# Two blocks of q and k in one load each, turned by head: one pair of a 24-block attention and FFN kernel

## The chip, the cores and the metric

The kernel runs on one core of a Trainium2 chip. The metric is the device time in microseconds (us), the median of several executions; beside it stands one execution that the hardware profiler recorded, on which the trace and the page are based.

## The reference

Two stages. The first is attention over 4 batches of 768 tokens with 8 heads of 64, where a query sees the last 96 keys and the first 8 of its batch, with a bias that falls with the distance at a slope of its own for each head. The second is a two-layer FFN with softplus over the 3072 rows of 512 that the attention gives.

```python
scores = scale * np.matmul(q, k.transpose(0, 1, 3, 2))
keep = is_global | is_local              # k < 8, or 0 <= q - k < 96
scores = np.where(keep, scores - slopes * dist, -1e9)
a = np.exp(scores - max);  a = a / (sum(a) + 1e-09)
attn = np.matmul(a, v)                   # 4 x 8 x 768 x 64
x = attn.transpose(0, 2, 1, 3).reshape(3072, 512)
h = x @ w_in                             # 512 -> 2048
g = np.maximum(h, 0.0) + np.log1p(np.exp(-np.abs(h)))
out = g @ w_out                          # 2048 -> 512
```

q, k, v and the weights come as float32; the matrices are multiplied in bf16 (attention) and fp16 (FFN).

## The kernel before, in words

**Attention** goes by blocks of 128 tokens, 24 of them, six to a batch. A block's q, k and v are loaded by `load` (L100): 128 tokens on the partitions, 8 heads of 64 beside each other, cast to bf16 on the way, in DMAs that POOL issues. `tr_qk` (L254, step `t`) turns q and k on PE, a pair of heads at a time as a 128x128 product with the identity, into one PSUM bank `tr`; `qt_copy` and `kt_copy` (steps `qc`, `kc`) bring it to SBUF as `QT` and `KT`. From block 8 on `dma_qk` (step `d`) has SP's queue do this by a DMA transpose instead. Only block 0 is loaded on the SP and ACT queues and cast on the chip (`cq`, `ck`, `tq`, `tk`).

A block is worked in two halves of four heads. For blocks 0 to 3 the bias is laid into PSUM by a product with the identity (`z`, L299), into the bank pair `s_ps` for heads 0 to 3 and `oo` for heads 4 to 7, and the scores (`s`, L321, made by `qk`, L277) are added on top of it; ACT takes the Exp straight from there (`e`). Each key block serves two query blocks, its own and the next. P.V is `p` (L367), the division by the sums `norm` (`nm`, two DVE instructions that write `xsf`), and the turned result goes to `XT`, for blocks 0 to 7 through PE (`x` and the copy `xc`), from block 8 on through a DMA transpose on SP's queue (`y`). The first 8 tokens of a batch are copied over rows of later key blocks by `gk` and `gv`. The number behind the dot in these steps is the half, and for the copies the engine: 0 DVE, 1 ACT, 2 POOL.

**The FFN** goes by chunks of 256 tokens, two blocks each, 12 of them. Chunks 0 and 1 are done directly: `f` (L428) is one group of 256 hidden columns, `fe` and `lp` its softplus on ACT, `o` the second layer. The other chunks use a seven-product scheme on half-size blocks: `ht` (`x_dif`, L503) makes differences of `XT` on DVE, `h` (L528) the products of the first layer, `hc`, `hv`, `he`, `hl` what follows them, `gs` sums of G on DVE, `m` (L645) the products of the second layer, `ec`, `ev` the evictions and `st` the stores on SP's queue.

**The order of the work** is written out by hand: the string `ORDER` (L707) names one step after another, and each step issues its instructions at once on its engines, in that order; `BANKS` (L187) says which of three PSUM banks each short-lived tile takes. An engine works its instructions strictly in the order given. POOL's DMAs go over eight semaphores in turn, so a load also waits until the eighth before it has landed. A load step `lq6` is q of block 6; `g` steps are tiny POOL copies that hold the loads behind them back until ACT has come to a certain place.

Of the kernel before, what the change touches and what calls it, by code (L numbers as in the profile page):

```python
# [10 lines left out]
ALU = mybir.AluOpType  # L11
# [9 lines left out]
def kernel(  # L21
# [51 lines left out]
    q_r = [const.tile([P, H, D], BF16, name=f"q_t{n}") for n in range(RQK)]  # L73
    k_r = [const.tile([P, H, D], BF16, name=f"k_t{n}") for n in range(RQK)]
# [42 lines left out]

    def load_q(n):
        load(n, q, q_t)

    def load_k(n):
        load(n, k, k_t)
# [56 lines left out]
    def bias_part(half, part):  # L179
# [8 lines left out]
        "01201201210212012012012012102101200220201011021010112121010212210101211202210221"  # L188
        "011020201002110121120202112001221002"
# [37 lines left out]
    def copy_by(act):  # L227
        return nc.scalar.copy if act else nc.vector.tensor_copy

    def to_QT(n, tr, copy):  # L230
        QT[n] = work4.tile([P, NPAIR, P], BF16, tag="QT", name="QT", bufs=6)
        copy(QT[n][:], tr[:, 0, :, :])
# [9 lines left out]
    def dma_qk(n):  # L242

        QT[n] = work4.tile([P, NPAIR, P], BF16, tag="QT", name="QT", bufs=6)
        KT[n] = work4.tile(
            [P, NPAIR, P], BF16, tag="KT0" if n == first_of(n) else "KT", name="KT",
            bufs=2 if n == first_of(n) else 6,
        )
        nc.sync.dma_start_transpose(QT[n][:], q_t[n][:].rearrange("p h d -> p (h d)"))
        nc.sync.dma_start_transpose(KT[n][:], k_t[n][:].rearrange("p h d -> p (h d)"))  # L250
# [7 lines left out]

    def qt_copy(n, by_act=0):
        to_QT(n, TR[n], copy_by(by_act))  # L260

    def kt_copy(n, by_act=0):
        to_KT(n, TR[n], copy_by(by_act))
# [239 lines left out]
    def x_dif(c, i):  # L503
# [8 lines left out]
        nc.vector.tensor_tensor(HD[c, i][:], a, b, ALU.subtract)  # L512
# [89 lines left out]
    def w_dif_part(i, part):  # L602
# [9 lines left out]
        nc.vector.tensor_tensor(t[i], a, b, ALU.subtract)  # L612
# [5 lines left out]
    def g_sum(c, i):  # L618
# [8 lines left out]
        nc.vector.tensor_tensor(SM[c, i][:], a(), b(), op)  # L627
# [74 lines left out]
    def gate(s):  # L702
# [5 lines left out]
        cq0 lk1 w18 bb1.1 ck0 tq0 lq1 lv0 lk2 tk0 z0.0 lq2 z0.1 lv1 lq3 s0.0 s0.1 bb1.0 bb0.1  # L708
        e0.1 t1 qc1.0 kc1.0 lk3 bb0.0 lv2 z1.1 e0.0 p0.1 s1.1 z1.0 s1.0 e1.1 nm0.1 gk2.1 t2 e1.0
        lk4 p0.0 z2.0 nm0.0 lq4 lv3 qc2.0 p1.1 wi1 p1.0 wi3 kc2.0 nm1.0 wi0 nm1.1 gv2.2 x0 s2.0  # L710
        z2.1 s2.1 t3 e2.0 z3.0 e2.1 gk3.2 p2.0 qc3.0 kc3.0 nm2.0 s3.0 p2.1 lk5 xc0.0 gv3.2 z3.1
        e3.0 s3.1 gk4.2 e3.1 nm2.1 x1 x2 t4 lq5 wi2 p3.0 xc1.0 lv4 wi4 p3.1 qc4.0 kc4.1 f1 xc2.1
        fe1 nm3.0 wo0 nm3.1 s4.0 lv5 x3 wi6 f3 xc3.0 fe3 f9 ab4.0 s4.1 fe9 ab4.1 f0 wo1 t5 kc5.0
        e4.0 f8 qc5.0 gk5.1 s5.0 fe0 f2 ab5.0 f11 fe8 e4.1 gv4.0 wo2 fe2 e5.0 s5.1 fe11 f10 lp0
        p4.0 f13 hw1.0 fe10 hw2.0 f5 fe13 f4 lp1 nm4.0 p4.1 ab5.1 fe4 nm4.1 e5.1 fe5 hw3.0 f12
        gv5.2 x4 p5.0 lp4 nm5.0 o0 p5.1 lq6 nm5.1 xc4.0 lk6 hw1.1 wo3 fe12 o4 x5 f15 xc5.0 lp6
        wd1.0 f14 lp5 f7 ht2.1 fe14 fe15 lk7 h2.1.0 ht2.2 lq7 o1 hw4.0 wd1.1 fe7 hw3.1 hw2.1 lv6
        ht2.4 lq8 hc2.1.0.1 hw4.1 f6 h2.6.0 lp7 gs1.1 wd3.0 gs1.3 h2.2.0 fe6 lp2 o5 gs1.2 ht2.3
        h2.5.0 lp3 hc2.5.0.1 lk8 lk9 o2 o6 he2.11.0 hv2.6.0 t6 lv7 kc6.1 wd2.0 wd4.0 h2.7.0 o7
# [24 lines left out]
        h5.4.0 ec3.4.1 ac14.0 he5.12.0 h5.1.1 hl4.1.1 he5.21.0 g37 lq16 y12 m3.2.0 lv15 nm13.1
        hc5.1.1.1 e14.1 gs4.1 ev3.2 lq17 ab14.0 h5.5.1 h5.2.1 gv14.2 hc5.5.1.1 h5.6.1 hv5.6.1
        he5.11.1 y13 gk15.2 gs4.3 st2.0 m4.1.0 e14.0 ss15 hl5.0.0 h5.7.1 h5.3.1 gk16.2 ec4.1.1
        lq18 ac15.0 p14.0 d16 he5.12.1 gs4.2 hv5.7.1 ac15.1 h6.1.0 hl5.0.1 gv13 g43 nm14.0
        hc6.1.0.1 lk18 gs5.3 m4.6 ht6.1 ec4.6.1 ht6.3 h5.4.1 he5.21.1 he5.22.1 m4.2.1 g31 p14.1
        h6.2.0 he6.11.0 lv17 ht6.2 d17 ab15.0 m4.7 gs4.4 h6.5.0 nm14.1 g29 h6.6.0 ev4.2 he5.22.0
# [52 lines left out]
    def cast_q(n):  # L802
        nc.vector.tensor_copy(q_t[n][:], q_f)
# [68 lines left out]
```

## Time and profile before

| | |
|---|---|
| median of the runs | 202.66 us (202.66, 202.66 and 203.97) |
| the profiled execution | 203.91 us, its span 201.8 us |
| granted TensorE clock | 0.997 |
| PE busy | 194.4 us, 96% |
| DVE, ACT busy | 173.8 and 173.5 us, 86% each |
| POOL busy | 85.3 us, 42% |
| DMA packets | 110622, 101760 of them under 512 B |

The span runs from the first to the last instruction of the profiled execution, and 2.1 us of its time lie around it. In rows of the trace a line is that of the kernel file, `out<-in` names the tiles, and a time in brackets is how long the engine had stood before the first instruction of the row, with what it had waited for. The length of a PE row holds the way of the last product through the array, so rows overlap; what a product costs in a stream is read from the start of one row to the start of the next.

### The profile page before, as it was taken

What the parts mean: (1) busy time and instruction counts of PE and PEld (TensorE: products, weight loads), DVE (VectorE), ACT (ScalarE), POOL (GpSimd) and SP (SyncE); (2) the same over time, 40 slices, a digit from 0 to 9 for tenths busy, and PEclk for the clock granted to TensorE, in tenths of its full rate; (3) what the DMA queues carried; (4) which work ended last, traced back from release to release, by engine and by line L of the source; (5) the groups of instructions that cost most, each with busy time, mean ns of one, the idle gap of its engine ahead of it and who ended that gap; (6) DMA issues with size and microseconds to landing.
All of it is one profiled execution on the core that took longest, in us unless ns stands there. A gap on an engine that the chain in (4) does not pass through costs nothing.

```text
span 201.8 us, 6676 instructions
## 1 busy us (share of the span) xinstructions
PE 194.4 (96%) x2729; PEld 167.9 (83%) x2729; DVE 173.8 (86%) x403; ACT 173.5 (86%) x278; POOL 85.3 (42%) x142
## 2 busy tenths in 40 slices
PE   7989999999999999999999999989999999999993
PEld 2657887867989989989998998969999999999992
DVE  7557776999999999989999999979999998867571
ACT  2767699989999999999999999997999998898700
POOL 8997906860574648095264835451003110000000
PEclk9999999999999999999999999999999999999998
DMA  8999999999999999999999999999442512601123
GB/s 126 153 156 169 149 196 207 188 173 158 149 115 157 120 174 195 102 158 158 157 161 180 168 177 167 100 119 145 100 133 44 94 29 30 209 3 54 54 71 138
DMA packets 110622, 26.91 MB, mean 133 GB/s; under 512 B 101760, under 2 KB 108288, under 8 KB 110592
## 3 DMA queue, kind: packets, MB, share of 16 engines
q0 software_dynamic: 78080, 13.37, 98.3%
q1 hardware_dynamic: 31472, 12.85, 36.8%
q8 instruction: 21, 0.34, 0.7%
q10 hardware_dynamic: 1040, 0.26, 0.6%
q14 instruction: 9, 0.07, 0.2%
HBM read 27.26 MB, written 6.29 MB: 166 GB/s over the span
## 4 chain that ended last, share of the span: by engine, by line
PE 59%; DVE 20%; ACT 11%; DMA 5%; issue 3%; DVEq 0%; ACTq 0%
PE o L657 24%; PE hT L541 12%; PE p_ps L541 6%; PE hT L434 5%; PE x_ps L380 3%; DMA XT<-xsf 3%; ACT e_sb L571 3%; DVE sum L627 3%; ACT Pb L364 3%; PE s_ps L284 2%; DVE Z L353 2%; DMA k_f<-in_k_dram 2%; ACT G L575 2%; DVE w_dif L612 2%; DVE xsf L398 2%
## 5 line engine op out<-in xcount | busy, mean ns | idle before, releaser
L575 ACT ACTIVATE G<-e_sb 128x1024 f16<-128x1024 f32 x40 | 41.7, 1061 | 0.1
L541 PEld LDWEIGHTS <-w_sum 128*128 128x128 f16 x640 | 39.0, 98 | 3.2 <-issue 0.9
L364 ACT ACTIVATE Pb<-Z 128x1024 bf16<-128x1024 f32 (+1 forms) x40 | 39.9, 1002 | 0.0
L657 PEld LDWEIGHTS <-sum 128*128 128x128 f16 x352 | 32.7, 98 | 4.3 <-issue 0.6
L657 PE MATMUL o<-w_dif,sum 128*128 128x256 f16 x264 | 33.8, 273 | 0.6 <-DVE b L686 0.5
L541 PEld LDWEIGHTS <-w_in 128*128 128x128 f16 x480 | 29.4, 98 | 0.7 <-DMA XT<-xsf 0.2
L657 PEld LDWEIGHTS <-G 128*128 128x128 f16 x272 | 24.9, 98 | 3.1 <-issue 0.2
L571 ACT ACTIVATE e_sb<-hT 128x512 f32<-128x512 f32 x40 | 24.0, 602 | 2.9 <-PE hT L541 2.6
L541 PE MATMUL hT<-x_dif,w_sum 128*128 128x128 f16 x320 | 24.4, 219 | 0.3 <-DVE hT L551 0.3
L541 PE MATMUL hT<-XT,w_in 128*128 128x128 f16 x320 | 24.4, 219 | 0.0
L344 DVE TENSOR_TENSOR Z<-s_ps,biasA 128x1024 f32<-128x1024 f32 x19 | 23.1, 1216 | 1.1 <-PE s_ps L284 1.1
L275 POOL COPY v_t<-v_t 8x520 bf16<-8x520 bf16 x13 | 8.4, 645 | 33.7 <-PE x_ps L380 32.6
L657 PE MATMUL o<-w_out,G 128*128 128x256 f16 x168 | 21.8, 273 | 0.0
L102 POOL DMA_DIRECT2D v_t<-in_v_dram x24 | 21.5, 896 | 0.6 <-issue 0.5
L102 POOL DMA_DIRECT2D q_t<-in_q_dram x23 | 20.6, 895 | 2.2 <-DMA w_out<-in_moe_w_out_dram 1.4
L102 POOL DMA_DIRECT2D k_t<-in_k_dram x23 | 20.6, 900 | 1.6 <-issue 0.8
L398 DVE TENSOR_TENSOR xsf<-x_ps,rcp 128x256 f16<-128x256 f32 x44 | 18.7, 424 | 1.5
L380 PEld LDWEIGHTS <-Pb 128*128 128x128 bf16 x352 | 15.3, 98 | 2.5 <-issue 0.9
L380 PE MATMUL x_ps<-v_t,Pb 128*128 128x65 bf16 x324 | 17.1, 193 | 0.1
L434 PE MATMUL hT<-XT,w_in 128*128 128x256 f16 x128 | 15.6, 273 | 0.0
L566 DVE TENSOR_TENSOR e_sb<-hp,hT 128x512 f32<-128x512 f32 x20 | 13.6, 682 | 2.3 <-PE hT L541 2.3
L627 DVE TENSOR_TENSOR sum<-G 128x1024 f16<-128x1024 f16 x22 | 15.1, 687 | 0.0
(113 smaller groups left out, 381.4 us busy)
## 6 DMA issues: line engine op xcount, KB each, us to landing
out_dram<-osb SPq DMA_DIRECT2D x18, 256.0 KB, 4.1
v_t<-in_v_dram POOLq DMA_DIRECT2D x24, 128.0 KB, 5.9
k_t<-in_k_dram POOLq DMA_DIRECT2D x23, 128.0 KB, 5.9
q_t<-in_q_dram POOLq DMA_DIRECT2D x23, 128.0 KB, 5.8
w_out<-in_moe_w_out_dram POOLq DMA_DIRECT2D x4, 512.0 KB, 11.2
out_dram<-osb SPq DMA_DIRECT2D x10, 128.0 KB, 2.0
w_in<-in_moe_w_in_dram POOLq DMA_DIRECT2D x4, 256.0 KB, 7.1
w_in<-in_moe_w_in_dram POOLq DMA_DIRECT2D x2, 512.0 KB, 9.1
```

The lines of the kernel that those rows point to most:

```text
L102: nc.gpsimd.dma_start(dst[n][:, :, 0:D], src[b, :, i * P : (i + 1) * P, :].rearrange("h s d -> s h d"))
L344: nc.vector.tensor_tensor(Z[:], buf[:, 0:8, :], biasA[:, half, :, :], ALU.add)
L364: nc.scalar.activation(Pb[:, 0:nreg, :], src, AF.Exp, scale=inv_sqrt)
L380: nc.tensor.matmul(x_b[:, lh, :], Pb[:, r, :], v_t[n - t][:, h, :], start=(t == 0), stop=(t == 1 or first),)
L398: nc.vector.tensor_tensor(xsf[:, h0 : h0 + 4, :], x_b[:, :, 0:D], rcp[:, h0 : h0 + 4][:, :, None].to_broadcast([P, 4, D]), ALU.mult,)
L434: nc.tensor.matmul(hT[:, j, :], w[:, m, fo : fo + P], XT[c][:, m, :], start=(j == 0 and m == 0), stop=(m == KM - 1), skip_group_check=(j > 0),
L541: nc.tensor.matmul(o[:, b, :], lhs(k, b), rhs[:, k, :], start=(i in (1, 5) and b == 0 and k == 0), stop=(k == KH - 1), skip_group_check=True,)
L566: nc.vector.tensor_tensor(t, HS[c, "p", u][:], HT[c, "x", u][:], ALU.add)
L571: nc.scalar.activation(o, t, AF.Exp)
L575: nc.scalar.activation(g_tile(c)[:, b0 : b0 + HB, :], HS.pop((c, i, u))[:], AF.Ln, bias=1.0)
L627: nc.vector.tensor_tensor(SM[c, i][:], a(), b(), op)
L657: nc.tensor.matmul(o, lhs[:, k, :], rhs(k)[:, c0:c1], start=(i in (1, 2, 5) and k == 0), stop=(k == NU - 1), skip_group_check=(i not in (1 ...
```

## The change

q of blocks 2 and 3 (tokens 256 to 511 of the first batch) is loaded in one DMA, and so is k. Partition s of the tile holds the neighbouring tokens 2s and 2s + 1, so that for each head 128 numbers lie together in memory rather than 64. The tiles of q and k are made for two blocks each, and the tiles of the single blocks are halves of them. Such a pair can't be turned two heads at a time; `tr_pair` turns it by head and by token parity, 16 transposes of 128x64 for q and as many for k, where two blocks had 8 for q and 8 for k. The copy to `QT` and `KT` (`out_of`) puts the two parities back together: it reads the PSUM bank in steps, 64 tokens of one and 64 of the other parity in turn. The arithmetic is the same.

`ORDER` and `BANKS` are new as a whole. The steps are the same but for `lq3`, `lk3`, `t2` and `t3`, which are gone, and `tQ2` and `tK2`, which are new; some 30 small copies have moved between ACT, DVE and POOL. `sum_by` lets three kinds of sums run on POOL, but no step asks for it.

```diff
-    q_r = [const.tile([P, H, D], BF16, name=f"q_t{n}") for n in range(RQK)]
-    k_r = [const.tile([P, H, D], BF16, name=f"k_t{n}") for n in range(RQK)]
+    q_p = [const.tile([P, 2 * H, D], BF16, name=f"q_t{n}") for n in range(RQK // 2)]
+    k_p = [const.tile([P, 2 * H, D], BF16, name=f"k_t{n}") for n in range(RQK // 2)]
+    q_r, k_r = ([t[n // 2][:, H * (n % 2) : H * (n % 2) + H, :] for n in range(RQK)] for t in (q_p, k_p))
...
+    PAIRED = (2,)
+
+    def pair_of(t, n):
+        return t[n % RQK // 2][:].rearrange("p (h t) d -> p h t d", t=2)
+
+    def load_pair(n, src, t):
+        b, i = divmod(n, BPB)
+        nc.gpsimd.dma_start(
+            pair_of(t, n), src[b, :, i * P : (i + 2) * P, :].rearrange("h (s t) d -> s h t d", t=2)
+        )
+
     def load_q(n):
-        load(n, q, q_t)
+        if n in PAIRED:
+            load_pair(n, q, q_p)
+        else:
+            load(n, q, q_t)
...
+    def tr_pair(n, t, which):
+        tr = TR[which, n] = any_bank([P, 2, NPAIR, P], BF16, f"tr_{which}")
+        src = pair_of(t, n)
+        for j in range(2):
+            for h in range(H):
+                rows = slice(D * (h % 2), D * (h % 2) + D)
+                nc.tensor.transpose(tr[rows, j, h // 2, :], src[:, h, j, :], ident[:])
+
+    def out_of(which, n, copy):
+        half = P // 2 * (n % 2)
+        src = TR[which, n - n % 2][:, :, :, half : half + P // 2].rearrange("p t m s -> p m s t")
+
+        return lambda dst, _: copy(dst.rearrange("p m (s t) -> p m s t", t=2), src)
...
-        cq0 lk1 w18 bb1.1 ck0 tq0 lq1 lv0 lk2 tk0 z0.0 lq2 z0.1 lv1 lq3 s0.0 s0.1 bb1.0 bb0.1
-        e0.1 t1 qc1.0 kc1.0 lk3 bb0.0 lv2 z1.1 e0.0 p0.1 s1.1 z1.0 s1.0 e1.1 nm0.1 gk2.1 t2 e1.0
+        lk1 cq0 w18 bb1.0 lq1 z0.1 lq2 ck0 tq0 lv0 bb1.1 z0.0 tk0 s0.1 e0.1 lk2 s0.0 t1 kc1.0
+        lv1 qc1.0 lk4 z1.1 tQ2 s1.1 bb0.1 qc2.0 lq4 p0.1 e0.0 qc3.0 bb0.0 lv2 e1.1 p0.0 z1.0 wi1
...
```

209 lines of the change are left out of this document (110 added, 99 removed).

## The prediction

> **What bounds the kernel now.** I read the windows first, stage by stage. Columns: length, busy time (and count) of PE, of its weight loads, of DVE, of ACT and of POOL, then clock, mean DMA engines at work, GB/s.
>
> ```profile
> 0.00:10.00 10.00, 8.56 (x49) 4.15 (x51) 6.34 (x33) 5.22 (x12) 9.09 (x15) 1.00 1.60 139
> 10.00:20.00 10.00, 9.22 (x153) 6.40 (x150) 6.64 (x23) 6.73 (x9) 8.65 (x14) 1.00 1.91 163
> 20.00:50.00 30.00, 29.82 (x347) 23.00 (x345) 25.71 (x56) 26.76 (x43) 16.04 (x20) 1.00 1.70 179
> 50.00:130.00 80.00, 79.26 (x1253) 72.18 (x1248) 77.78 (x170) 78.24 (x127) 43.49 (x76) 1.00 1.89 154
> 130.00:140.00 10.00, 9.14 (x147) 8.14 (x145) 8.30 (x20) 8.65 (x13) 4.72 (x9) 1.00 2.09 137
> 140.00:190.00 50.00, 50.00 (x721) 46.65 (x719) 43.19 (x93) 46.70 (x76) 3.30 (x10) 1.00 0.29 70
> 190.00:201.80 11.80, 8.44 (x86) 7.40 (x83) 5.90 (x14) 1.21 (x3) 0.00 (x0) 0.96 0.32 113
> ```
>
> PE is the bound from 20 us to 190 us: it idles 0.18 + 0.74 + 0.86 + 0 = 1.8 us in 170. The last stretch ends with the same products, evictions and stores in both orders. So a new order can win at most those 1.8 us, and whatever the first 20 us hold; there POOL is the busiest engine (9.09 and 8.65 of 10), because it issues the loads one after another.
>
> Then PE, ACT and POOL in order of time through that head (start, length, instructions):
>
> ```profile
> 0.78 4.00 PE L800 MATMUL x_ps<-const-bfloat16-1.0 128*128 128x512 bf16 x9 [0.78 <-PEq L853]
> 5.35 0.61 PE L223 MATMUL tr<-ident,q_t 128*128 128x128 bf16 x4 [0.58 <-DVE q_t L803]
> ...
> 7.98 0.61 PE L223 MATMUL tr<-ident,q_t 128*128 128x128 bf16 x4
> 8.38 0.63 PE L223 MATMUL tr<-ident,k_t 128*128 128x128 bf16 x4
> 8.81 1.00 PE L310 MATMUL oo<-biasA,ident 128*128 128x512 bf16 x2
> 9.64 0.29 PE L380 MATMUL x_b<-v_t,Pb 128*128 128x65 bf16 x4
> 9.87 0.40 PE L284 MATMUL oo<-QT,KT 64*128 64x128 bf16 x8
> 10.20 0.60 PE L310 MATMUL s_ps<-biasA,ident 128*128 128x512 bf16 x2
> 10.74 0.40 PE L284 MATMUL s_ps<-QT,KT 64*128 64x128 bf16 x8
> 11.07 0.40 PE L223 MATMUL tr<-ident,q_t 128*128 128x128 bf16 x4
> 11.30 0.39 PE L223 MATMUL tr<-ident,k_t 128*128 128x128 bf16 x4
> 11.52 0.29 PE L380 MATMUL x_ps<-v_t,Pb 128*128 128x65 bf16 x4
> 12.41 0.59 PE L310 MATMUL s_ps<-biasA,ident 128*128 128x512 bf16 x2 [0.60 <-ACT Pb L364]
> 12.84 0.40 PE L380 MATMUL x_b<-v_t,Pb 128*128 128x65 bf16 x8
> 19.25 1.04 PE L434 MATMUL hT<-XT,w_in 128*128 128x256 f16 x8
> 20.23 0.40 PE L284 MATMUL s_ps<-QT,KT 64*128 64x128 bf16 x8
> ```
>
> Lengths hold the drain, so costs are read from start to start. Two bias products took 0.83 (8.81 to 9.64), later 0.54 (10.20 to 10.74) and 0.43 (12.41 to 12.84): PE runs at half rate until about 9.8, though the granted clock reads 1.00. Four transposes took 0.43 then (8.38 to 8.81), and 0.23 and 0.22 at full rate: 0.107 and 0.056 us each. The 0.11 between 0.54 and 0.43 is what changing between whole-array products and the 64-row ones of the scores costs.
>
> ```profile
> 10.31 1.03 ACT L364 ACTIVATE Pb<-oo 128x1024 bf16<-128x1024 f32 x1 [0.53 <-PE oo L284]
> ...
> 14.15 1.02 ACT L364 ACTIVATE Pb<-s_ps 128x1024 bf16<-128x1024 f32 x1 [1.78 <-PE s_ps L284]
> ...
> 17.92 1.02 ACT L364 ACTIVATE Pb<-oo 128x1024 bf16<-128x1024 f32 x1
> 2.37 0.88 POOL L102 DMA_DIRECT2D q_t<-in_q_dram  x1
> ...
> 11.90 2.33 POOL L108 DMA_DIRECT2D w_in<-in_moe_w_in_dram  x3
> ```
>
> The head is one chain: load, transposes, copy, bias and scores on PE, Exp on ACT (1.02 each), the bank free again for the next bias.
>
> **The change part by part: loads.** Four issues of 0.88 become two. A w_in issue steps 0.74 for 256 KB against 0.88 for 128 KB, so issue time goes by pieces, not bytes; a pair has as many pieces as one block had (128 by 8). I take 0.88 a pair: 1.75 us of POOL saved (none, if it went by bytes). Landing, from the tile views of q_t up to 12 us and of w_in up to 14 us:
>
> ```profile
> DMA to landing us min/median/max: 4.5/4.6/4.6
> DMA to landing us min/median/max: 6.8/7.3/7.9
> ```
>
> Counting on from 2.37, the q pair is issued at 3.24 and lands between 7.8 (as q_t) and 10.5 (as w_in); I take 8.3, nearer the rows with equally many small pieces. The first w_in, now tenth in the queue instead of thirteenth, goes out at 9.30 instead of 11.90 and lands 2.6 us sooner. But PE idles 0.18 us in 20 to 50, so earlier weights are worth 0.2 at most later on.
>
> **Transposes.** 16 of 128x128 become 32 by head, each half as wide in its weights and still 128 columns long: 32 x 0.056 − 16 x 0.056 = +0.9, and four changes of tile shape at 0.11, +0.4. The trace has no transpose of 64 columns; the ends are 0.041 (eight 64-row scores in 0.33, 9.87 to 10.20) and 0.107 each. I take 0.056, the same operation. What counts is where they stand. On PE, between the bias of block 1's second half (z1.1) and its scores (s1.1), before:
>
> ```order
> L310 LDWEIGHTS ident
> L310 MATMUL oo<-biasA,ident 128x512
> ...
> L380 LDWEIGHTS Pb
> L380 MATMUL x_b<-v_t_90,Pb 128x65
> ...
> L284 LDWEIGHTS KT
> L284 MATMUL oo<-QT,KT 128x128
> ```
>
> And in the changed kernel (q_t_79 is the second pair's tile, tr_q its PSUM bank):
>
> ```order
> L351 LDWEIGHTS ident
> L351 MATMUL oo<-biasA,ident 128x512
> ...
> L286 LDWEIGHTS q_t_79
> L286 MATMUL tr_q<-ident,q_t_79 64x128
> ...
> L325 LDWEIGHTS KT
> L325 MATMUL oo<-QT,KT 128x128
> ```
>
> Four short products have made way for 16 transposes, so s1.1 waits for them, and behind it the Exp. Nothing hides that. Walking the chain: z1.1 ends at 9.64 as now; transposes 0.9 + 0.2 to 10.7; scores 0.33; Exp at 11.2 (now 10.31) and 12.3, ending 13.3. The k pair's transposes stand behind s1.0, from 12.1 to 13.2; their copy for block 2 comes on DVE after two norms, and is done at 13.8. From 13.3 PE does both P.V halves of block 1 (0.5), both bias pairs of block 2 (0.87) and the first scores (0.33): Exp at 15.1 (now 14.15), the next at 16.1, block 3's at 18.1 and 19.1 (now 17.92). Against that, the first FFN group (f1, 0.87) now stands ahead of block 3's P.V: 18.7 to 19.6, then p3.0, x2, p3.1 after the Exp's end at 20.1, and s4.0 at 20.5. It starts at 20.23 now, with the same PE work behind it. **Head: +0.3.** The ends: if full rate comes before 8.8, z1.1 and half a block's transposes save 0.8 (−0.5); if half rate lasts to 13, both groups of 16 cost 0.8 more each and bias and scores between them 0.5 (+2.4).
>
> The four copies out of the pairs' banks read PSUM in steps:
>
> ```profile
> L232 DVE COPY QT<-tr 128x512 bf16<-128x512 bf16 x6 | 2.5, 421 | 3.0 <-PE tr L223 3.0
> L554 DVE COPY hp<-p_ps 128x512 f32<-128x512 f32 x5 | 3.4, 684 | 0.3 <-PE p_ps L541 0.3
> ```
>
> Each costs 0.42 to 0.68; only block 2's KT is on the chain, so at most +0.26, inside the bounds above.
>
> **The middle.** DVE's only waits for a DMA of XT are these two, and the longer lies in the one bad window, 130 to 140:
>
> ```profile
> DVE x_dif L512 <- DMA XT<-xsf: 2.0, 2, 1.4
> 125.76 0.42 DVE L398 TENSOR_TENSOR xsf<-x_ps,rcp 128x256 f16<-128x256 f32 x1
> 126.22 0.69 DVE L353 TENSOR_TENSOR Z<-s_lo,biasA 128x512 f32<-128x512 f32 x1
> ...
> 127.42 1.22 DVE L344 TENSOR_TENSOR Z<-s_ps,biasA 128x1024 f32<-128x1024 f32 x1
> ...
> 130.64 0.68 DVE L566 TENSOR_TENSOR e_sb<-hp,hT 128x512 f32<-128x512 f32 x1
> 132.69 0.29 DVE L512 TENSOR_TENSOR x_dif<-XT 128x256 f16<-128x256 f16 x1 [1.37 <-DMA XT<-xsf]
> ```
>
> Block 17's xsf is done at 126.2, DVE is through its other work at 131.3 and stands 1.37: 5.1 us of work did not cover the DMA transpose. The landings, from the tile view of XT on SP's queue at 126.2 and at 114 to 121:
>
> ```profile
> DMA to landing us min/median/max: 6.4/6.4/6.4
> DMA to landing us min/median/max: 4.3/5.2/6.0
> ```
>
> DVE's rows between block 17's xsf and its x_dif, before:
>
> ```order
> L353 TENSOR_TENSOR Z_2863<-s_lo_2846,biasA_123 128x512
> L353 TENSOR_TENSOR Z_2863<-o_2847,biasA_123 128x512
> L344 TENSOR_TENSOR Z_2908<-s_ps_150,biasA_123 128x1024
> L566 TENSOR_TENSOR p5_ps_2881<-hp_2910,hT_2816 128x512
> L627 TENSOR_TENSOR sum2_2919<-sum1_2856,G_2668 128x1024
> L395 RECIPROCAL rcp_2956<-x_ps_151 128x4
> L398 TENSOR_TENSOR xsf_2955<-x_ps_151,rcp_2956 128x256
> L696 TENSOR_TENSOR osb_2757<-a_2535,o_2927 128x256
> L566 TENSOR_TENSOR e_sb_2976<-hp_2910,hT_2816 128x4x128
> L512 TENSOR_TENSOR x_dif1_2995<-XT_2753 128x256
> ```
>
> In the changed kernel 14 rows stand there for block 17, worth 6.7 us by the same steps, enough for 6.4. The tightest is now block 15:
>
> ```order
> L385 TENSOR_TENSOR Z_2614<-s_ps_144,biasA_117 128x1024
> L607 TENSOR_TENSOR p5_ps_2498<-hp_2534,hT_2542 128x512
> L727 COPY b_2619<-o_2551 128x256
> L668 TENSOR_TENSOR sum4_2665<-G_2207,sum2_2577 128x1024
> L436 RECIPROCAL rcp_2668<-x_ps_145 128x4
> L439 TENSOR_TENSOR xsf_2667<-x_ps_145,rcp_2668 128x256
> L607 TENSOR_TENSOR e_sb_2681<-hp_2534,hT_2542 128x4x128
> L727 COPY u_2684<-o_2551 128x256
> L737 TENSOR_TENSOR osb_2695<-u_2684,o_2568 128x256
> L436 RECIPROCAL rcp_2668<-x_ps_145 128x4
> L439 TENSOR_TENSOR xsf_2667<-x_ps_145,rcp_2668 128x256
> L553 TENSOR_TENSOR x_dif1_2700<-XT_2460 128x256
> ```
>
> In steps from start to start (0.6 for 512 f32, from the two between 126.22 and 127.42; 0.35 for 256 and 0.2 for a reciprocal, from 125.76 to 126.22 and the sum of what stands up to 130.64; that leaves 1.1 for a full Z) this is 5.05 us. Against the 5.2 of its neighbourhood it just fits; against 6.4 it stands 1.4. Block 17's wait goes, and with it most of the 0.86 PE lost in its window; I keep 0.15 for block 15. **Middle: −0.7**; the ends are −1.8 (all PE idle time after 20 us) and +1.0 (blocks 9 and 15 both stand as 17 did).
>
> **Sum.** On the profiled execution's 203.91 us: +0.3 − 0.7 = 203.5. That execution was 1.25 above the median of the runs shown, 202.66, so the forecast is 202.3.
>
> **The rivals.** *Slower, the head at half rate:* transposes now fill much of PE's time between 8 and 13 us, and full rate may come later. For it: with 8 transposes in 5.35 to 6.7 and 8 more at 7.98, full rate came only at 9.8, after 9 us of PE work that began at 0.78. Against: bias products, scores and P.V stand between them. It decides if half rate outlasts about 12 us; then the head costs +2.4 and the middle gives nothing: 202.66 + 2.4 = 205.1. Chance 0.13. The Trainium skill, "TensorE: Matmul & The Clock Gate", Part 4 (PE-mode transpose), says that a transpose does not count as a busy PE in the same way, so that the full clock does not engage on it; by that rule this rival would be the likeliest, while the trace, whose last slow stretch was half transposes and still ended in full rate, does not settle it. *Faster, everything falls right:* full rate before 8.8 (z0.1, a bias that needs no load, now follows the warm-up products at once, where PE stood 0.58) and no DVE wait left: −0.5 − 1.8 = 200.4. Chance 0.17. *No gain in the middle:* block 15 or 9 takes over the wait: 202.66 + 0.3 + 0.3 = 203.3. Chance 0.25. The forecast's own case has 0.45.
>
> **How the numbers follow.** Within 1% of 202.66 (about what a measurement of this kernel can tell, its runs spread 0.65%) means 200.6 to 204.7. The slower rival lies outside; the faster one mostly does, with some of the forecast's spread: faster 0.19, same 0.68, slower 0.13. The range reaches to the faster rival, 200.4, and to 204.9, just short of the slower one, which leaves out about a tenth on each side.
>
> **What would show it.** Right: the Exp of block 1 starts near 11.2 and that of block 2 near 15.1, s4.0 near 20.5, the first w_in is issued near 9.3; PE loses under 0.4 us in 130 to 140 and DVE's wait for XT is under 1 us. Wrong: bias products of 0.4 us each after 10 us (half rate lasted), transposes by head far from 0.056 us, a wait of PE for the pair's landing at 9.6, or PE idle over 2.5 us between 20 and 190 for a cause not named here.

## The result, and the profile after

In the first comparison the changed kernel takes 200.52 us (200.16 to 200.85, 4 runs) against 203.12 (202.66 to 203.97, 4 runs): a ratio of 0.987, 95% interval 0.982 to 0.991. Put beside the kernel before twice more, it takes 201.92 against 203.03 us, 0.9965 (0.993 to 1.000), and 201.57 against 203.15, 0.9936 (0.990 to 0.997). It is faster, by 0.4% to 1.3%, with some 0.5% as the better supported figure. One execution differs from the next by up to 2% (the kernel before: 201.31 to 205.43 in 35 runs), so much below rests on traces and not on times alone. The ratios leave out the slow executions (over 1.5% above the fastest of their kernel), so they are not quite the quotients of the medians beside them.

The windows of the changed kernel, stage by stage (columns as in the prediction; the last but one is not a number of engines but the time of all packets as a share of the 16 DMA engines' time, and passes 1 where packets overlap):

```profile
0.00:10.00 10.00, 8.54 (x72) 4.47 (x73) 6.42 (x34) 5.38 (x13) 9.10 (x15) 1.00 1.43 147
10.00:20.00 10.00, 9.25 (x156) 6.46 (x155) 7.20 (x25) 8.70 (x13) 8.58 (x12) 1.00 2.05 172
20.00:50.00 30.00, 29.98 (x347) 23.46 (x346) 25.45 (x54) 27.33 (x43) 14.82 (x21) 1.00 1.63 181
50.00:130.00 80.00, 79.22 (x1261) 72.86 (x1259) 78.04 (x174) 78.97 (x128) 44.40 (x75) 1.00 1.90 154
130.00:140.00 10.00, 10.00 (x166) 9.39 (x164) 9.73 (x23) 9.95 (x20) 3.63 (x6) 1.00 2.07 171
140.00:190.00 50.00, 50.00 (x713) 46.69 (x711) 43.23 (x93) 44.09 (x71) 2.84 (x9) 1.00 0.29 70
190.00:198.40 8.40, 5.09 (x47) 4.30 (x45) 2.59 (x7) 0.74 (x2) 0.00 (x0) 0.95 0.26 94
```

PE idles 0.02 + 0.78 + 0 + 0 = 0.8 us between 20 and 190, where it was 1.8, and nothing in 130 to 140, where it was 0.86. PE's rows through the head in order of time (start, length, instructions):

```profile
7.54 0.40 PE L241 MATMUL tr<-ident,q_t 128*128 128x128 bf16 x4
7.78 0.39 PE L241 MATMUL tr<-ident,k_t 128*128 128x128 bf16 x4
8.19 0.59 PE L351 MATMUL oo<-biasA,ident 128*128 128x512 bf16 x2
8.71 0.64 PE L286 MATMUL tr_q<-ident,q_t 128*64 128x128 bf16 x16
9.28 0.40 PE L325 MATMUL oo<-QT,KT 64*128 64x128 bf16 x8
19.02 0.40 PE L325 MATMUL s_ps<-QT,KT 64*128 64x128 bf16 x8
```

The Exp of blocks 1 and 2 on ACT, and POOL's first issue of w_in, in the same view:

```profile
9.73 1.02 ACT L405 ACTIVATE Pb<-oo 128x1024 bf16<-128x1024 f32 x1
13.66 1.02 ACT L405 ACTIVATE Pb<-oo 128x1024 bf16<-128x1024 f32 x1 [0.68 <-PE oo L325]
...
9.42 0.80 POOL L109 DMA_DIRECT2D w_in<-in_moe_w_in_dram  x1
```

Two bias products take 0.52 us from start to start at 8.19, and four transposes 0.24 at 7.54: PE works at its full rate by then, where the kernel before was at half rate and took 0.43 for four at 8.38. The 16 transposes by head take 0.57 (8.71 to 9.28). The Exp of block 1 starts at 9.73 (10.31 before), that of block 2 at 13.66 (14.15), and block 4's first scores, s4.0, at 19.02 (20.23).

What is left of waits for a DMA transpose after 20 us, a row of DVE and one of PE in order of time:

```profile
73.71 0.29 DVE L553 TENSOR_TENSOR x_dif<-XT 128x256 f16<-128x256 f16 x1 [0.39 <-DMA XT<-xsf]
72.17 0.62 PE L582 MATMUL hT<-XT,w_in 128*128 128x128 f16 x8 [0.60 <-DMA XT<-xsf]
```

PE stands 0.60 at 72.17, for the transposes of chunk 4's blocks. The first trace of the kernel before has no stand there, but the stand is not new: a later trace of the same kernel (e5, below) has 0.69 at the same products, and two others with the old order behind block 4's first scores have 0.17 (e7) and 0.91 (e8).

```profile
73.47 0.62 PE L541 MATMUL hT<-XT,w_in 128*128 128x128 f16 x8 [0.69 <-DMA XT<-xsf]
```

### The profile page after: what moved, and what is told of

It reads as the page before. It is cut to its first block, busy times and chain, and to the rows that moved or that the text cites. A ratio compares the mean times of both kernels' runs of the same rounds, so it can differ in the third digit from the quotient of the medians.

```text
span 198.4 us, 6719 instructions
## 1 busy us (share of the span) xinstructions
PE 192.1 (97%) x2743; PEld 167.6 (84%) x2745; DVE 172.7 (87%) x404; ACT 175.2 (88%) x283; POOL 83.4 (42%) x134
## 4 chain that ended last, share of the span: by engine, by line
PE 86%; DMA 6%; POOL 2%; DVE 2%; issue 1%; ACT 1%; POOLq 0%; ACTq 0%
PE o L698 33%; PE hT L582 22%; PE p_ps L582 8%; PE hT L475 7%; PE x_ps L421 5%; PE o L627 3%; PE s_ps L325 3%; DMA XT<-xsf 3%; DMA v_t<-in_v_dram 3%; PE s_lo L325 1%; ACT Pb L405 1%; PE tr L241 1%; PE tr_x L454 1%; DVE Z L394 1%; POOL k_t L103 1%
## 5 line engine op out<-in xcount | busy, mean ns | idle before, releaser
L616 ACT ACTIVATE G<-e_sb 128x1024 f16<-128x1024 f32 x40 | 42.2, 1064 | 0.1
L316 POOL COPY v_t<-v_t 8x520 bf16<-8x520 bf16 x11 | 7.2, 652 | 31.0 <-PE x_ps L421 29.6
L103 POOL DMA_DIRECT2D k_t<-in_k_dram x21 | 18.8, 895 | 1.1 <-DMA w_out<-in_moe_w_out_dram 0.8
L103 POOL DMA_DIRECT2D q_t<-in_q_dram x21 | 18.7, 893 | 1.1 <-issue 1.1
L421 PEld LDWEIGHTS <-Pb 128*128 128x128 bf16 x352 | 15.1, 97 | 2.3 <-issue 0.6
L668 DVE TENSOR_TENSOR sum<-G 128x1024 f16<-128x1024 f16 x22 | 15.1, 685 | 0.5 <-ACT G L616 0.4
L607 DVE TENSOR_TENSOR p_ps<-hp,hT 128x512 f32<-128x512 f32 x20 | 13.8, 690 | 1.2 <-ACT hp L595 0.6
```

Source lines behind the costliest of these rows:

```text
L103: nc.gpsimd.dma_start(dst[n][:, :, 0:D], src[b, :, i * P : (i + 1) * P, :].rearrange("h s d -> s h d"))
L421: nc.tensor.matmul(x_b[:, lh, :], Pb[:, r, :], v_t[n - t][:, h, :], start=(t == 0), stop=(t == 1 or first),)
L607: nc.vector.tensor_tensor(t, HS[c, "p", u][:], HT[c, "x", u][:], ALU.add)
L616: nc.scalar.activation(g_tile(c)[:, b0 : b0 + HB, :], HS.pop((c, i, u))[:], AF.Ln, bias=1.0)
L668: sum_by(by)(SM[c, i][:], a(), b(), op)
```

## The experiments

From here on two numbers of each trace are set beside each other: when s4.0 starts (the head), and how long it is from there to the end of the last product (the middle). PE works without a gap from 190 us on, so 190 and its busy time in the last window give that end: 195.09 by the row above, 198.44 before. The moment of full rate is read, to about half a microsecond, from the first group of four 128x128 transposes that is 0.40 long and not 0.61, or within the warm-up products from the time they took together. In the kernel before it is read from the two bias products that take 0.83 us from 8.81 to 9.64, where two later ones take 0.54 or less: half rate lasts to their end, and full rate comes at about 9.6.

| kernel | ratio to before (95%) | median, runs | full rate from about | s4.0 | s4.0 to the end of PE |
|---|---|---|---|---|---|
| before (the page) | 1 | | 9.6 | 20.23 | 178.2 |
| changed (first trace) | 0.987 (0.982 to 0.991) | 200.52, 4 | 6.3 | 19.02 | 176.1 |
| e1, changed | 0.9965 (0.993 to 1.000) | 201.92, 12 | 6.6 | 19.95 | 177.6 |
| e2, z0.1 put back | 0.994 (0.991 to 0.997) | 201.52, 12 | 6.1 | 19.74 | 176.4 |
| e3, single loads | 0.994 (0.991 to 0.997) | 201.26, 12 | 5 | 19.93 | 175.8 |
| e4, before, longer warm-up | 0.998 (0.995 to 1.001) | 202.78, 12 | 3.6 | 19.40 | 178.8 |
| e5, before | 1.000 (0.996 to 1.003) | 202.52, 10 | 5 | 19.11 | 178.3 |
| e6, old head, new middle | 0.995 (0.993 to 0.998) | 201.98, 12 | 5 | 19.12 | 177.4 |
| e7, new head, old middle | 1.000 (0.997 to 1.002) | 202.86, 12 | 6.6 | 19.11 | 178.3 |
| e8, before, x_dif later | 0.995 (0.992 to 0.998) | 201.54, 12 | 4.5 | 19.11 | 177.5 |
| e9, changed | 0.994 (0.990 to 0.997) | 201.57, 11 | 3.9 | 19.83 | 176.9 |
| e10, changed, PE swap | 0.994 (0.992 to 0.997) | 201.71, 12 | 6.6 | 19.73 | 176.1 |
| e11, e10 with single loads | 0.992 (0.988 to 0.995) | 201.05, 6 | 5 | 19.84 | 175.8 |
| e12, before with the pairs | 1.008 (1.004 to 1.012) | 204.53, 7 | 5 | 21.50 | 178.7 |

The first question was which part made the head 1.2 us shorter: the loads by pairs, or full rate at 6.3 rather than 9.6 us, and whether the stand of 0.58 us after the warm-up products had to do with the rate.

**The changed kernel again (e1).**

> The changed kernel as it is, beside the three below on one chip, as their base. Both theories: 0.985 to 0.990 of the kernel before (200.2 to 201.0 us); four 128x128 transposes at 7.5 take 0.24 us, the 16 by head at 8.7 take 0.57, block 4's first scores start at 19.0, PE idles under 0.3 us in 130 to 140. If the switch to full rate is a matter of luck from one execution to the next, it comes elsewhere than at 6.4 us here.

Its ratio missed what was expected, and so did s4.0: 19.95, with PE at full rate from about 6.6, as in the first trace. That trace's short head is not the kernel's own: its first loads of k and q on POOL landed 4.2 and 4.0 us after their issue, here 5.0 and 4.9. The k pair landed 5.6 us after its issue there and 6.4 here, and PE now stands for it:

```profile
11.46 0.64 PE L286 MATMUL tr_k<-ident,k_t 128*64 128x128 bf16 x16 [0.46 <-DMA k_t<-in_k_dram]
```

**The gap put back (e2).**

```
-  lk1 cq0 w18 bb1.0 lq1 z0.1 lq2 ck0 tq0 lv0 bb1.1 z0.0 tk0 s0.1
+  lk1 cq0 w18 bb1.0 lq1 lq2 ck0 tq0 lv0 bb1.1 z0.0 tk0 z0.1 s0.1
```

> The changed kernel with one step moved: the bias of block 0's second half (z0.1), which follows the warm-up products at once, stands again behind the transposes of block 0, so that PE stands some 0.5 us after the warm-up, as in the kernel before. Nothing else moves. Theory 'the gap': the unbroken run of products is what brings full rate at 6.4 us; with the gap it comes near 9.8, two bias products at 8.2 take 0.83 again and not 0.52, the 16 transposes by head take 1.0 or more and not 0.57, block 4's first scores start at 19.8 to 20.3 and not at 19.02, and the kernel takes 0.7 to 1.3 us longer than the changed one. Rival 'the order': the rate doesn't hang on the gap, all these stay within 0.2, and the time within 0.2.

PE's rows with the gap:

```profile
5.36 0.61 PE L241 MATMUL tr<-ident,q_t 128*128 128x128 bf16 x4 [0.58 <-DVE q_t L844]
6.17 0.39 PE L241 MATMUL tr_k<-ident,k_t 128*128 128x128 bf16 x4
8.65 0.64 PE L286 MATMUL tr_q<-ident,q_t 128*64 128x128 bf16 x16
19.74 0.40 PE L325 MATMUL s_ps<-QT,KT 64*128 64x128 bf16 x8
```

The gap is back (0.58), yet four transposes at 6.17 have the length of full rate, 0.39 and not 0.61, and the 16 take 0.57 again (the next row starts at 9.22). The theory of the gap fell. The late s4.0, 19.74, which it had foretold, is no sign for it, since e1 without the gap has 19.95; the time is 0.4 us under e1's, where the rival allowed 0.2.

**Single loads in the new order (e3).**

```
-        nc.gpsimd.dma_start(pair_of(t, n), src[...])      # two blocks in one load
+        for j in range(2):
+            load(n + j, src, q_t if t is q_p else k_t)
...
-                nc.tensor.transpose(tr[rows, j, h // 2, :], src[:, h, j, :], ident[:])
+            tr_in(tr, j, (q_t if which == "q" else k_t)[n + j])
```

> The changed kernel with its order kept, but q and k of blocks 2 and 3 loaded one block a DMA (two of them where the pair's load stands), turned two heads at a time, 8 transposes of 128x128 where 16 by head stand, and copied plainly. Theory 'pairs': POOL is 1.75 us later from the k load on, the k of block 3 lands near 12.2 and not 10.57, PE stands 1 to 1.5 us for it at 10.7, the Exp of block 2 starts at 14.5 to 15 and not 13.66, block 4's first scores at 19.5 to 20.2, and the kernel takes 0.5 to 1.3 us longer than the changed one. Rival 'order': the gain is the new order's alone, in the clock and in the middle; the time is within 0.3 of the changed kernel's.

It is not slower: 201.26 us beside 201.92 of e1 on the same chip, 0.66 lower where the rival 'order' allowed 0.3, with s4.0 at 19.93 beside 19.95. So the pairs bring nothing in this order. Where POOL's 1.75 us went is seen in the landings. The tile view of k_t in the changed kernel (e9, below), for the pair, issued at 4.97:

```profile
DMA to landing us min/median/max: 6.0/6.0/6.0
```

And in e3, for the two single loads, issued at 5.95 and 6.82:

```profile
DMA to landing us min/median/max: 4.5/4.5/4.6
```

The pair lands at 4.97 + 6.0 = 10.9, the second single load at 6.82 + 4.5 = 11.4. The first w_in is issued 1.7 us earlier with pairs (9.43 in e9 against 11.14) and lands 0.5 earlier (15.7 against 16.2). The DMA engines are the likely reason. Their busy tenths over the first 20 us, in 40 slices, and what they moved, in the kernel before:

```profile
DMA  0000599999999999999999999999999999999999
DMA packets 17176, 3.02 MB, mean 151 GB/s; under 512 B 15663, under 2 KB 17175, under 8 KB 17175
```

And in the changed kernel:

```profile
DMA  0001999999999999999999999999999999999999
DMA packets 16387, 3.18 MB, mean 159 GB/s; under 512 B 14879, under 2 KB 16386, under 8 KB 16386
```

From 2.5 us on they have packets under way in every slice, with either kernel, at 151 GB/s before and 159 after. The landings fit that. In the first trace of the changed kernel the q pair lands 1.9 us after the load issued ahead of it and the k pair 1.3 us, a single load 0.7 to 1.0 us; and the single loads behind the pairs land 5.2 to 5.6 us after their issue, where those of the kernel before take 4.5 to 4.8. So what POOL hands over sooner stands in line. No run tested this apart from the order of the loads.

**A longer warm-up in the kernel before (e4).**

```
-  cq0 lk1 w18 bb1.1 ck0 tq0
+  cq0 lk1 w20 bb1.1 ck0 tq0
```

> The kernel before with ten warm-up products where it had nine, so that PE works to about 5.0 us instead of 4.6 and stands 0.15 to 0.35 us for block 0's q, not 0.58. Nothing else moves. Theory 'the gap': full rate by 6.5 to 7.5 us, the four k transposes at 8.4 take 0.23 and not 0.43, the bias products behind them 0.54 and not 0.83, the Exp of block 1 starts near 9.8 and not 10.31, block 4's scores 0.3 to 1.0 earlier than 20.23; time 0.3 to 1.0 us under the kernel before. Rival 'the order': full rate stays at 9.8, or it comes and the w_in transfers, unchanged at 18.7, hold the head at 20.2; time within 0.2.

PE's rows:

```profile
0.78 3.69 PE L800 MATMUL x_ps<-const-bfloat16-1.0 128*128 128x512 bf16 x10 [0.78 <-PEq L853]
5.35 0.40 PE L223 MATMUL tr<-ident,q_t 128*128 128x128 bf16 x4 [0.87 <-DVE q_t L803]
19.40 0.40 PE L284 MATMUL s_ps<-QT,KT 64*128 64x128 bf16 x8
```

The first row is the warm-up. Its ten products take less than nine took (3.69 against 4.00), so full rate came at about 3.6, inside the warm-up and before the edit could have brought it. The head is 0.83 shorter (19.40), and the time the same within its interval: the middle took 178.8. Neither theory told of that; the trace suggested that the moment of full rate is chance, and that the gain lies in the middle. The second group was made for these two.

**The kernel before again (e5).**

> The kernel before as it is, for a second trace of it. Theory 'phase': the moment of full rate is free from one execution to the next (seen so far at 9.8 in this kernel, at about 6.4, 6.7, 6.1, 5.0 and 4 in five others, with and without a stand of PE after the warm-up), so it comes somewhere between 4 and 10 us here, most likely not at 9.8 again; from block 4's first scores to the last product it is 178.0 to 179.0 us as before (178.2). Rival 'gap': the old order stands 0.58 at 4.79 and again 0.27 before the k transposes, so full rate comes at 9.8 again. Time: 1.00 of itself, within 0.004.

PE's rows:

```profile
5.35 0.40 PE L223 MATMUL tr<-ident,q_t 128*128 128x128 bf16 x4 [0.57 <-DVE q_t L803]
7.29 0.40 PE L223 MATMUL tr<-ident,q_t 128*128 128x128 bf16 x4
19.11 0.40 PE L284 MATMUL s_ps<-QT,KT 64*128 64x128 bf16 x8
```

And its last window, by which PE ends at 197.44:

```profile
190.00:200.80 10.80, 7.44 (x76) 6.51 (x74) 5.35 (x13) 0.74 (x2) 0.00 (x0) 1.00 0.27 99
```

The same program, with the same stand of 0.57, has full rate at 5.35: four transposes have a length of 0.40 there, where the first trace still showed 0.61 at 7.98. Its s4.0 comes at 19.11, 1.1 us sooner than in the first trace. So the moment of full rate is free from one execution to the next, and the 20.23 of the first trace was late by chance.

**Old head, new middle (e6).** The kernel before up to s4.0; behind it every step that is left, in the changed kernel's order, with its engines and PSUM banks.

```
   ...the order of the kernel before, to:   wo0 nm3.0 ... nm3.1 s4.0
-  lv5 x3 wi6 f3 xc3.0 fe3 f9 ab4.0 s4.1 fe9 ab4.1 f0 wo1 ...
+  gv4.1 f3 x3 ab4.0 t5 fe3 xc3.0 e4.0 s4.1 f9 lv5 ab4.1 ...
```

> The kernel before up to block 4's first scores (s4.0), single loads and all, and from there the steps in the changed kernel's order, with its engines and banks. Theory 'middle': what the change wins, it wins behind s4.0: from s4.0 to the last product it takes 175.8 to 177.6 us and not 178.2, PE loses under 0.3 in 130 to 140, DVE doesn't wait for block 17's transpose; time 1.0 to 2.0 us under the kernel before. Rival 'head': the gain is in the loads, the transposes and the rate of the head; the time is within 0.4 of the kernel before.

It is faster, by 0.8 us in the median, with the head of the kernel before, though by less than the 1.0 to 2.0 of the theory. From s4.0 on it takes 177.4, at the upper end of what was expected: the seam, the place where the two orders are joined, costs it a stand of its own, as q of block 5 is not there yet when t5 comes. From PE's waits (in total, times, longest):

```profile
PE tr L222 <- DMA q_t<-in_q_dram: 1.0, 1, 1.0
```

**New head, old middle (e7).** The seam the other way round.

```
   ...the order of the changed kernel, to:   x2 fe1 p3.1 xc2.1 s4.0
-  gv4.1 f3 nm3.0 nm3.1 x3 ab4.0 t5 wo0 fe3 xc3.0 e4.0 s4.1 ...
+  nm3.0 wo0 nm3.1 lv5 x3 wi6 f3 xc3.0 fe3 f9 ab4.0 s4.1 ...
```

> The changed kernel up to block 4's first scores (s4.0), pairs and all, and from there the steps in the order of the kernel before. Theory 'middle': from s4.0 to the last product 178.0 to 179.0 us, DVE waits over 1 us for block 17's transpose, PE loses over 0.8 in 130 to 140; time within 0.5 of the kernel before, since two heads at equal rate end at the same 19.4 to 20.0. Rival 'head': 0.8 to 1.5 us under the kernel before.

DVE's row at block 17's wait:

```profile
131.64 0.29 DVE L552 TENSOR_TENSOR x_dif<-XT 128x256 f16<-128x256 f16 x1 [0.78 <-DMA XT<-xsf]
```

And the window around it:

```profile
130.00:140.00 10.00, 9.48 (x150) 8.68 (x148) 8.87 (x22) 8.79 (x15) 4.64 (x9) 1.00 1.64 133
```

No gain: 1.000, a middle of 178.3, and in 130 to 140 PE idles 0.52 us behind DVE's wait of 0.78, both somewhat less than expected. Of the two halves, the new middle has the gain and the new head with its pairs has none.

**Block 17's wait alone (e8).**

```
-  g41 m6.6 h7.4.1 ht8.1 ht8.2 he7.21.1 hc8.1.0.0 e19.1 p18.1 m6.2.1 h8.5.0 d20 hc8.5.0.1 gs6.3
+  g41 m6.6 h7.4.1 he7.21.1 hc8.1.0.0 e19.1 p18.1 m6.2.1 gs6.3 ht8.1 ht8.2 h8.5.0 d20 hc8.5.0.1
```

> The kernel before with three of DVE's steps moved: the differences of XT for chunk 8 (ht8.1, ht8.2), which wait for block 17's DMA transpose, and a sum of G (gs6.3) stand a few steps later, so that DVE does a copy of 0.7 us and the sum before it waits. Nothing else moves. Theory 'block 17': this wait is what costs PE its time at 134 to 136; DVE's wait falls from 1.4 to under 0.4, PE's loss in 130 to 140 from 0.86 to under 0.3, and the kernel is 0.4 to 0.9 us faster. Rival: PE's products of chunk 8 need these differences at once, so they wait as long as DVE did, and the time is within 0.2.

DVE's rows where it had waited:

```profile
131.43 0.68 DVE L627 TENSOR_TENSOR sum<-G 128x1024 f16<-128x1024 f16 x1
132.03 0.28 DVE L512 TENSOR_TENSOR x_dif<-XT 128x256 f16<-128x256 f16 x1
```

And the window:

```profile
130.00:140.00 10.00, 10.00 (x162) 9.29 (x160) 9.57 (x23) 9.50 (x17) 4.82 (x9) 1.00 1.89 128
```

After the sum DVE finds XT there, and PE idles 0 us in the window. The kernel before with this one edit is 0.5% faster (0.2% to 0.8%), about as much as with the whole change in e1 and e9 (0.35% and 0.64%), though not as in the first comparison (1.3%). The middle is 0.9 us shorter than e5's, while PE's stand for XT at 73 is 0.2 longer. The rival, by which PE waits for the differences all the same, fell. What the wait had cost is read from the same products without it:

```profile
132.40 0.61 PE L541 MATMUL p_ps<-x_dif,w_sum 128*128 128x128 f16 x8
134.11 1.03 PE L657 MATMUL o<-w_dif,sum 128*128 128x256 f16 x8
```

Four groups take 1.71 us here, from the first row's start to the second's.

The last group asked whether the changed kernel's stand at 72 can be removed, and what the pairs do by themselves.

**The changed kernel, base of the last group (e9).**

> The changed kernel as it is, beside the three below on one chip, as their base. 0.987 to 0.997 of the kernel before; from block 4's first scores to the last product 175.8 to 177.6 us, PE stands 0.6 to 0.8 us at 72 to 73 for the DMA transpose of block 8.

As expected in ratio and middle; PE's stand at 72 was 0.43 here, less than expected. PE also stood 0.42 for the q pair at 8.71, and 0.44 at 142.31 for a DMA transpose of k.

**Chunk 4's first products later on PE (e10).**

```
-  ss11 p10.0 lq13 ac11.1 h4.1.0 h3.4.1 ac11.0 nm10.0 e10.1 ht4.1 m2.4 lk15
+  ss11 p10.0 lq13 ac11.1 h3.4.1 m2.4 h4.1.0 ac11.0 nm10.0 e10.1 ht4.1 lk15
```

> The changed kernel with three of PE's steps in another order: the first products of chunk 4 (h4.1.0), which read block 8's XT straight from its DMA transpose, stand behind a group of chunk 3's (h3.4.1) and m2.4 and not ahead of them, 1.3 us of work. Nothing else moves. Theory 'landing': PE's stand of 0.6 to 0.8 us at 72 goes, and nothing waits for h4.1.0 itself; from block 4's first scores to the last product 0.5 to 0.8 us less than the changed kernel, which shows in the time, 0.003 to 0.004 of it. Rival: what follows h4.1.0 (its copy, the next products) is needed as soon, and PE stands as long a few steps later; time the same.

PE's rows:

```profile
72.34 0.61 PE L582 MATMUL hT<-x_dif,w_in 128*128 128x128 f16 x8
73.77 0.61 PE L582 MATMUL hT<-XT,w_in 128*128 128x128 f16 x8
76.98 0.61 PE L582 MATMUL hT<-x_dif,w_sum 128*128 128x128 f16 x8 [0.17 <-DVE x_dif L553]
```

The stand at 72 is gone, and a shorter one, 0.17, has come at 76.98, behind DVE's wait for the other transpose of that chunk. The middle is 176.1 us beside 176.9 of e9, but e9's holds the stand of 0.44 at 142, which this trace does not have; the time shows nothing of it (201.71 beside 201.57). Whether some tenths were won can't be said at this spread.

**The same with single loads (e11).**

> The kernel of the run above, with q and k of blocks 2 and 3 loaded one block a DMA and turned two heads at a time, as in the third experiment. Theory 'the pairs bring nothing' (a pair lands 1.3 to 1.9 us after the load ahead of it, a single block 0.85, so two singles land when the pair does): time within 0.4 us of the run above. Rival 'pairs': 0.5 to 1.3 us longer than it.

201.05 us, 0.992: the lowest median of its group, 0.66 under e10 where the theory allowed 0.4, with an interval that overlaps those of e9 and e10. The rival fell. It stands beside e10 as e3 beside e1, 0.66 us lower in both cases. Why single loads should be the better is not settled: the heads are alike (19.84 and 19.73), and the middles of e3 and e11 (175.8) are at the low end of the spread of the others.

**The pairs alone in the kernel before (e12).**

```
-  tk0 z0.0 lq2 z0.1 lv1 lq3 s0.0 ... kc1.0 lk3 bb0.0 ... gk2.1 t2 e1.0 ... qc2.0 ... kc2.0 ... s2.1 t3 e2.0 ... qc3.0 kc3.0
+  tk0 z0.0 lq2 z0.1 lv1 s0.0 ... kc1.0 bb0.0 ... gk2.1 tQ2 tK2 e1.0 ... qc2.0 qc3.0 ... kc2.0 kc3.0 ... s2.1 e2.0 ...
```

> The kernel before with the pairs alone: one load for q of blocks 2 and 3 where q of block 2 was loaded, one for k likewise, transposes by head where block 2's stood, the strided copies, and all else in the old order. Theory 'the pairs bring nothing': POOL issues the first w_in 1.75 us earlier, but the pair lands as late as two single loads, and PE's wait at block 2 is ACT's, not a load's; time within 0.4 us of the kernel before, block 4's first scores at 19.0 to 19.8, from there 178.0 to 179.0 to the last product. Rival 'pairs': 0.8 to 1.8 us faster. Another rival, 'cost': the transposes by head and the strided copies (0.5 to 0.68 each on DVE) lie on the chain, 0.5 to 1.0 slower.

Theory and first rival missed. The kernel is slower, as the rival 'cost' has it, but by 0.8%, 1.4 us in the median, where that rival had 0.5 to 1.0; block 4's scores start at 21.50, 2.4 us after e5's. PE's rows at the pairs, and one of its waits:

```profile
11.40 0.64 PE L285 MATMUL tr_q<-ident,q_t 128*64 128x128 bf16 x16 [1.35 <-DMA q_t<-in_q_dram]
11.87 0.61 PE L285 MATMUL tr_k<-ident,k_t 128*64 128x128 bf16 x16
...
PE tr_x L453 <- DVE QT L291: 0.8, 1, 0.8
```

The q pair, issued at 4.95 behind the k pair, lands 6.4 us after its issue by the tile view, where the single block of q that e5 issues at 4.97 takes 4.4, and PE stands 1.35 us for it; it stands another 0.8 for DVE's strided copies of QT, which come two in a row. The two stands together are 2.1 of the 2.4 us, the landing first. The transposes by head are no part of it: the 16 for q, with 16 of the same shape behind them, take 0.47 us (11.40 to 11.87). In the changed kernel the q pair is the third load on POOL. Neither wait is among PE's in its first trace, but shorter stands for a pair are there in e1 (0.46) and e9 (0.42).

Behind s4.0 this kernel has the old order, and it shows what block 17's wait hangs on. Its DMA transpose landed 4.3 us after issue here and not 6.4, DVE did not stand for it, and PE idles 0 us in 130 to 140. The middle is 178.7 even so, with stands of PE elsewhere: 0.65 for w_in at 37.51, and 0.85 at 92.64 behind DVE's wait for a transpose of chunk 5.

## Why the prediction was right, and where it was not

The forecast was 202.3 us, 0.4 under the median shown, in a range of 200.4 to 204.9. The first comparison, 200.52, is at the range's lower end, with 0.1 to spare, at the time of the rival "everything falls right" (200.4); the two later ones, 201.92 and 201.57, lie 0.4 and 0.7 under the forecast. As a ratio to the kernel before, 0.998 was forecast and 0.987, 0.9965 and 0.9936 were measured.

**Loads: right in the issue, not in what follows a pair.** The first w_in went out at 9.42 (forecast 9.30), and the q pair landed 5.0 us after its issue, at 8.3, as forecast. That earlier weights would be worth next to nothing held too: e3, where they come later, is no slower. But the sum gave nothing for the loads behind a pair. They land up to 1 us later after their issue than before, and PE's stands for a pair in e1 (0.46) and e9 (0.42) are of the kind that the prediction names among its signs of being wrong. The column read as "mean DMA engines at work" is a share of all 16 engines' time: at 1.6 in the first 10 us they had on average more than one packet each under way, and were not mostly idle, as that name suggests.

**Transposes: the step that failed is "I take 0.056, the same operation".** They took 0.57 / 16 = 0.036 us each, in a stream that still holds a change of shape, below the lower end of 0.041. From the tile view:

```profile
L286 PE MATMUL tr_q<-ident,q_t x16: 219/220/243, 8.7 to 9.1; 128*64 128x128 bf16 x16
L241 PE MATMUL tr<-ident,q_t x8: 218/260/315, 5.3 to 7.7; 128*128 128x128 bf16 x8
```

By these rows a product by head is as long (220 ns) as one of 128x128 at full rate (218), but they start closer together: 0.036 against 0.060 (0.24 / 4, at 7.54). The Trainium skill, "TensorEngine Tiling (Array Packing)", Key Properties, says that tiles of the array can load weights and multiply independently and in parallel; two halves of 64 columns that are used in turn, at 0.036 each, agree with that. So each group cost 0.57 where the prediction had 0.9 + 0.2; it was some 0.5 too dear each time. Without a change of shape behind them, in e12, 16 take 0.47, as much as the eight of 128 columns that they replace (twice 0.23 to 0.24).

**The head: +0.3 was near right as a mean, in part by luck.** Six traces with the new head and the pairs have s4.0 at 19.02, 19.95, 19.74, 19.11, 19.83 and 19.73, on average 19.56; five of the old head at 20.23, 19.40, 19.11, 19.12 and 19.11, on average 19.39. That is +0.2, or +0.4 without the old head at 20.23, with a spread that is larger. The walk's own marks missed: Exp of block 1 near 11.2, of block 2 near 15.1, s4.0 near 20.5, where the first trace has 9.73, 13.66 and 19.02. Too dear transposes and a half rate that was not there made the walk long, and the old head of 20.23 that it was set against was long too, at least in part by that half rate, so the difference of the two came out. The step that failed here is "PE runs at half rate until about 9.8", which I took as a property of the kernel and of what stood on PE. It is one of an execution: 3.6 to 6.6 us in all the other traces, of both orders. Nor does the new head follow the rate from one trace to the next: with full rate from 3.9 s4.0 is at 19.83 (e9), with 6.3 at 19.02. It goes with the landing of the k pair, which no term of the sum holds: where that took 5.6 and 5.7 us (the first trace, e7) s4.0 is at 19.02 and 19.11, where it took 5.9 to 6.4 (e2, e9, e10, e1) at 19.73 to 19.95. This is read off six traces, and no run changed the landing alone. The Trainium skill, "TensorE: Matmul & The Clock Gate", Part 1, says that the window of about 3.4 us over which PE's activity is judged runs freely and does not start with the kernel, so that the number of slow products changes from run to run. The traces agree that the moment changes from run to run, with full rate from 3.6 us at the earliest and 9.6 at the latest; that is far more than the half microsecond to either side that the same part gives. Its Part 4, that transposes don't count as a busy PE, would have made the slower rival the likeliest. In no trace with transposes by head did half rate reach them, and that rival fell; the rule by itself was not tested.

**The middle: right in mechanism and place, too small in size.** The wait of block 17 was named as what costs the window 130 to 140, and e8 shows that it does. The 6.7 us of work that the prediction counted ahead of it hold too: in the first trace and e2 its transpose lands 6.1 and 6.6 us after issue and DVE doesn't stand, in e1 and e9 it takes 7.1 and 7.0 and DVE stands 0.48 and 0.28. Block 15, which "just fits", stands in no trace of the new order; the wait that is left in most of them, 0.39 at 73.71 in the first, is chunk 4's, as PE's is. But the sum took −0.7 and, as its lower end, "−1.8 (all PE idle time after 20 us)". On average the middle is 178.5 us in the old order (178.2, 178.8, 178.3, 178.3, 178.7) and 176.4 in the new (176.1, 177.6, 176.4, 175.8, 176.9, 176.1, 175.8), leaving out e6 with its seam and e8: −2.1. The bound was read from busy time, and that misses stands that lie under a row's length. PE in the kernel before, behind DVE's wait:

```profile
133.04 0.62 PE L541 MATMUL p_ps<-x_dif,w_sum 128*128 128x128 f16 x8
133.97 0.61 PE L541 MATMUL hT<-x_dif,w_sum 128*128 128x128 f16 x8 [0.31 <-DVE hT L551]
134.42 0.61 PE L541 MATMUL hT<-XT,w_in 128*128 128x128 f16 x8
135.11 0.40 PE L380 MATMUL x_ps<-v_t,Pb 128*128 128x65 bf16 x8
135.98 1.03 PE L657 MATMUL o<-w_dif,sum 128*128 128x256 f16 x8 [0.46 <-DVE b L686]
```

The four groups take 2.94 us from start to start (133.04 to 135.98), where e8, which has no such wait, takes 1.71 for the same four: 1.23 us lost, of which the busy time shows 0.86 in the whole window. A row of eight products is 0.61 long where the next follows after 0.45, so each of the three stands under these rows shows some 0.16 too short. Most of DVE's stand of 1.37 was thus passed on. So the term of −0.7 is the one that was mis-sized: with 1.2 in its place the forecast would have been 201.8, between the two later comparisons. Taking this wait alone away won 0.9 in e8's middle beside e5's, less than half of the 2.1. Of the rest the traces show a part: with the old order PE also stands behind ACT or DVE near 49, 60 and 107 us in every trace (0.18, 0.23 and 0.12 in the first; some 3 us later in e12), with the new one, 0.11 near 61 (and in e10 the 0.17 above). What else is in it stays open.

**The rivals.** "No gain in the middle" fell, and so did the slower one. The likeliest case had the mechanism; "everything falls right" had the size of the first comparison, but by a middle larger than its 1.8, beside a trace whose head was short by its landings.

## What to carry to other kernels

Read the loss of a bound engine from the starts of equal groups of instructions, not from its busy time: each row that holds a drain covers some 0.16 us of the stand behind it, and here that hid nearly a third of the loss. When a change has several parts, see which one the gain hangs on: here moving three steps of DVE, so that a DMA transpose had landed when it was needed, gave about as much time as a new load scheme and a new order together did in two of three comparisons, and the load scheme gave none. Fewer issues did not help where the DMA engines had packets under way throughout: the first w_in was issued 1.7 us sooner and landed 0.5 sooner. Call a stand new only after a second trace of the kernel before: the one at 72 was missing from the first by chance.

## What was not expected of the hardware

- Full rate of PE begins at another time in another execution of one and the same program, about 5 us after its start in one and 9.6 in another (e5 and the page), while the clock in the windows reads 1.00 throughout; the execution with the late one has s4.0 1.1 us later.
- Sixteen transposes of 64 columns, used in turn on the two halves of the array, take 0.47 us in a stream of their kind (e12) and 0.57 with a change of shape behind them; the eight of 128 columns that turn the same data take about 0.47 (twice 0.23 to 0.24).
- A load of two blocks lands 5.0 to 6.4 us after its issue and a single one at a like place in the queue 4.4 to 4.7, while the issue takes POOL 0.87 to 1.0 us for either.
